# Work buffers for weight sums in a fused attention, mixture-of-experts and Strassen kernel, and idle turnings ahead of its branches

## The chip, the cores and the metric

The kernel runs on one core of one Trainium2 chip. The metric is the device time of one execution in microseconds (us). A core has five engines with a queue of instructions each: TensorE (PE in the profile; PEld is its loading of weights), VectorE (DVE), ScalarE (ACT), GpSimd (POOL) and SyncE (SP, which mostly issues DMAs). An engine takes its instructions strictly in order and waits at one until the semaphores that it names have come. DVEq, ACTq and PEq in the profile are the instruction sequencers of these engines, which do branches, register loads and the issuing of DMAs.

## The reference

Three stages in a row, all in float32 (cut to what is computed):

```python
# 1. attention in chunks of 64 tokens, 8 batches x 8 heads, 576 tokens each, head size 64
x = softmax(q_c @ k_c.T / 8) @ v_c            # -> 4608 tokens x 512
# 2. eight experts; only tokens with x @ w_skip > 0 are computed
e_idx = argmax(xc @ w_gate); gate = softmax(xc @ w_gate)[e_idx]
for e in range(8):                            # w1[e]: 512 x 1024, w2[e]: 1024 x 512
    y[mask] = gate * (relu(xc[mask] @ w1[e]) @ w2[e])
x[do_compute] = xc + y
# 3. a maxout layer: w1, w2, w3 are 512 x 768, w_out is 768 x 512
h = max(relu(x @ w1), x @ w2, x @ w3)
return h @ w_out
```

How many tokens an expert gets is known only on the chip.

## The kernel before

Every float32 product is made of three matmuls (`mm3`): each operand is split into a high part `hi` and a rest `lo` of a reduced type, and hi·hi, hi·lo and lo·hi are added up in PSUM. For the weights of expert e the raw piece `raw_e` is loaded by SP, ScalarE casts it to `whi_e` (L90), and VectorE, or GpSimd for pieces 0 and 1, subtracts to get `wlo_e` (L91). There are eight pieces for each expert. Pieces 0, 1, 2, 3 and 7 of expert e+1 (`EARLY`) are written ahead of expert e's products, pieces 6, 4 and 5 (`LATE`) after its branch.

Phase 1 (to about 213 us of the trace) is attention and the sorting of tokens to experts. Phase 2 (213 to 530 us) runs the experts 0 to 7, here called e0 to e7. An expert does two tiles of 128 tokens without a question (`first_tiles`: 96 matmuls `h`, of 256 columns, that make the hidden layer; 12 turnings `trm`, transposes through TensorE that prepare the rows of the next tiles; then 48 matmuls `y` back). VectorE's put-back (L694, `xg<-y,xg`) ends a tile, and GpSimd writes its rows home. Then stands a branch, `tc.If(n_e > 256)` (L983; L989 for e7): a third tile (`single`) is done only if the expert has so many tokens, inside of it a fourth (L916), and inside of that a loop (L920, L921). [...] The third tile of e0 is done always. In the profiled execution the third tile was done by e0, e2, e3, e5 and e7, and the fourth by e2 and e3.

Phase 3 (530 to 1108 us) is the maxout layer in blocks of 1024 rows, with seven products of sums of weight quarters in place of eight. These sums (`n_q`, kept in DRAM as `m_sums`) are 18 steps called n_q0 to n_q17. Steps 0 to 10 are made during phase 2, beside the experts (`STEPS = [2, 2, 2, 2, 2, 1, 0, 0]` of them are written in e0 to e7), and 11 to 17 in the first block of phase 3. A step loads one raw block (`n_raw`, two buffers), narrows it from 64-bit to 32-bit values (L531 to L533 and L536 on VectorE, L534 on ScalarE), makes four sums (L569 to L572 on VectorE, 128x128), casts (L575 on ScalarE) and subtracts (L576 on VectorE, 128x896), and then ScalarE and SP each store one half (L577, L578). The buffer `n_q` of phase 2 is one (`bufs=1`), so that the first instructions of a step (L531, L534) wait until the store of the step before has landed. In the first block `m2_direct` narrows w_out in six pieces (`n_q_m`), with the buffers "s4" (two) that steps 11 to 17 use as well.

The order of the instructions on each engine comes from a scheduler that goes by the order of the program text and by the buffers that are free; the kernel pins some of it with `issue_after`.

## Time and profile before

| what | value |
|---|---|
| time, median of 3 runs | 1114.9 us (1110.21 to 1116.59) |
| the profiled execution: its time / its span | 1109.83 / 1108.1 us |
| mean granted clock of TensorE | 0.979 of full speed |
| busy share of the span: PE, DVE, ACT, POOL | 94%, 55%, 40%, 28% |
| phase 2, the eight experts | about 213 to 530 us |
| phase 3 | about 530 to 1108 us |

TensorE is at work in nearly all of the span. What can be won is where it stands still, and where it runs at half clock after it stood still. The averages over the whole span say little of single stages: VectorE, 55% busy over all, is 89% busy (23.11 of 26.00 us) in the stretch of expert e4.

### The profile page before, as it was taken

What the parts mean: (1) busy time and instruction counts of PE and PEld (TensorE: products, weight loads), DVE (VectorE), ACT (ScalarE), POOL (GpSimd) and SP (SyncE); (2) the same over time, 40 slices, a digit from 0 to 9 for tenths busy, and PEclk for the clock granted to TensorE, in tenths of its full rate; (3) what the DMA queues carried; (4) which work ended last, traced back from release to release, by engine and by line L of the source; (5) the groups of instructions that cost most, each with busy time, mean ns of one, the idle gap of its engine ahead of it and who ended that gap; (6) DMA issues with size and microseconds to landing.
All of it is one profiled execution on the core that took longest, in us unless ns stands there. A gap on an engine that the chain in (4) does not pass through costs nothing.

```text
span 1108.1 us, 17499 instructions
## 1 busy us (share of the span) xinstructions
PE 1042.2 (94%) x6320; PEld 872.1 (79%) x6320; DVE 614.8 (55%) x1299; ACT 446.2 (40%) x774; POOL 309.1 (28%) x297
## 2 busy tenths in 40 slices
PE   7899799988899998998899799999999999999997
PEld 6788677777788787887687588878888888788996
DVE  6687588756756477671499772335244442443241
ACT  6677487434434244431444342222322232223231
POOL 4124232364404044320432160222312140123021
PEclk9999799999899999999999999999999999999999
DMA  9999996257764468544898934663566545666591
GB/s 211 195 216 232 261 229 183 89 195 259 265 217 136 138 211 273 192 150 141 274 319 285 300 114 136 197 190 114 165 194 192 166 139 166 183 186 208 186 288 38
DMA packets 217513, 216.99 MB, mean 196 GB/s; under 512 B 50219, under 2 KB 179403, under 8 KB 217408
## 3 DMA queue, kind: packets, MB, share of 16 engines
q1 hardware_dynamic: 206384, 183.62, 57.3%
q0 software_dynamic: 8432, 23.76, 6.6%
q10 hardware_dynamic: 2592, 8.26, 1.9%
q8 instruction: 60, 0.98, 0.4%
q14 instruction: 45, 0.37, 0.1%
HBM read 175.15 MB, written 41.83 MB: 196 GB/s over the span
## 4 chain that ended last, share of the span: by engine, by line
PE 41%; DMA 6%; DVE 3%; issue 3%; POOL 1%; ACT 0%; SPq 0%; POOLq 0%; DVEq 0%; ACTq 0%
PE f_a L705 5%; PE f_a L707 5%; PE f_a L706 5%; PE o L705 4%; PE o L707 4%; PE o L706 4%; DMA ws<-m_sums 3%; PE f_d L705 3%; PE f_d L707 3%; PE f_d L706 3%; DMA m_sums<-n_q 2%; PE f_b L705 1%; PE f_b L707 1%; PE f_b L706 1%; PE trf L879 1%
## 5 line engine op out<-in xcount | busy, mean ns | idle before, releaser
L91 POOL TENSOR_TENSOR fh<-best,fh 128x512 fp32r<-128x512 f32 (+1 forms) x60 | 77.0, 1290 | 356.3 <-ACT fh L90 270.4
L705 PE MATMUL f_a<-x_t,ws 128*128 128x512 f32 (+1 forms) x270 | 100.7, 373 | 5.0 <-DVE p L1034 4.8
L706 PE MATMUL f_a<-x_t,ws 128*128 128x512 f32 (+1 forms) x270 | 99.9, 370 | 0.0
L707 PE MATMUL f_a<-x_t,ws 128*128 128x512 f32 (+1 forms) x270 | 99.7, 370 | 0.0
L90 ACT CAST whi_e<-raw_e 128x1024 fp32r<-128x1024 f32 x64 | 65.1, 1045 | 60.0 <-DMA raw_e<-in_moe_w_dram 34.8
L705 PE MATMUL h<-xhi,whi_e 128*128 128x256 f32 x256 | 75.5, 295 | 12.2 <-DVEq L983 7.0
L706 PE MATMUL o<-wlo_m,fh 128*128 128x512 f32 x216 | 84.6, 392 | 0.0
L705 PE MATMUL o<-whi_m,fh 128*128 128x512 f32 x216 | 83.4, 392 | 0.0
L707 PE MATMUL o<-whi_m,fh 128*128 128x512 f32 x216 | 83.4, 392 | 0.0
L91 DVE TENSOR_TENSOR wlo_e<-raw_e,whi_e 128x1024 fp32r<-128x1024 f32 x50 | 67.1, 1351 | 18.1 <-ACT whi_e L90 15.9
L705 PE MATMUL y<-whi_e,hhi 128*128 128x512 f32 x184 | 74.3, 406 | 2.6 <-ACT hhi L772 1.8
L707 PE MATMUL y<-whi_e,hlo 128*128 128x512 f32 x184 | 72.8, 400 | 1.8 <-DVE hlo L712 1.6
L706 PE MATMUL h<-xlo,whi_e 128*128 128x256 f32 x256 | 74.4, 291 | 0.0
L707 PE MATMUL h<-xhi,wlo_e 128*128 128x256 f32 x256 | 74.3, 290 | 0.0
L706 PE MATMUL y<-wlo_e,hhi 128*128 128x512 f32 x184 | 72.3, 395 | 0.0
L696 POOL DMA_INDIRECT x_dram<-xg,ids_sb x20 | 20.6, 1030 | 180.2 <-DVE xg L694 72.8
L90 ACT CAST fh<-best 128x512 fp32r<-128x512 f32 (+1 forms) x60 | 34.7, 579 | 89.5 <-DVE best L1036 57.9
L1039 ACT COPY p<-f_a 128x512 f32<-128x512 f32 (+1 forms) x45 | 24.5, 545 | 99.3 <-PE f_a L707 99.1
L705 PEld LDWEIGHTS h<-xhi,whi_e 128*128 128x128 f32 x256 | 51.0, 199 | 15.3 <-ACTq L983 6.3
L705 PEld LDWEIGHTS f_a<-x_t,ws 128*128 128x128 f32 x270 | 51.2, 190 | 14.5 <-DVE p L1034 5.3
L707 PEld LDWEIGHTS f_a<-x_t,ws 128*128 128x128 f32 x270 | 51.2, 190 | 8.6
L706 PEld LDWEIGHTS f_a<-x_t,ws 128*128 128x128 f32 x270 | 51.2, 190 | 8.3
(226 smaller groups left out, 2678.7 us busy)
## 6 DMA issues: line engine op xcount, KB each, us to landing
ws<-m_sums SPq DMA_DIRECT2D x135, 512.0 KB, 5.2
raw_e<-in_moe_w_dram SPq DMA_DIRECT2D x64, 512.0 KB, 5.1
ws<-m_sums SPq DMA_DIRECT2D x45, 256.0 KB, 3.9
v_bd<-in_v_dram SPq DMA_DIRECT2D x144, 64.0 KB, 4.2
x<-x_dram SPq DMA_DIRECT2D x36, 256.0 KB, 4.9
out_dram<-os SPq DMA_DIRECT2D x36, 256.0 KB, 2.0
x_dram<-xg SPq DMA_DIRECT2D x17, 512.0 KB, 4.2
m_sums<-n_raw ACTq DMA_DIRECT2D x18, 448.0 KB, 6.0
```

The lines of the kernel that those rows point to most:

```text
L90: nc.scalar.copy(hi, src),
L91: eng.tensor_tensor(lo, src, hi.bitcast(F32), op=ALU.subtract),
L696: ins = nc.gpsimd.indirect_dma_start(out=x_dram[:, :], out_offset=bass.IndirectOffsetOnAxis(ap=ids, axis=0), in_=xg, in_offset=None, bound ...
L705: nc.tensor.matmul(acc, ahi, bhi, start=first, stop=False, skip_group_check=onto)
L706: nc.tensor.matmul(acc, ahi, blo, start=False, stop=False, skip_group_check=onto)
L707: return nc.tensor.matmul(acc, alo, bhi, start=False, stop=last, skip_group_check=onto)
L879: nc.tensor.transpose(tr[:, i * P:(i + 1) * P], row[:, c * P:(c + 1) * P], ident)
L1039: nc.scalar.copy(p1, acc_a)
```

## The change

It has four parts. `n_q` of phase 2 gets two buffers. To make room, the raw pieces of weights that go through the pool `mpool` have one buffer in place of two, and piece 1 goes through the other pool, whose three buffers it shares with pieces 2, 7 and `LATE`. The narrowing of w_out (`m2_direct`) gets a buffer of its own, one, in place of the two of "s4". And after the last `y` matmul ahead of each branch TensorE does eight turnings of the constant `ident` into a PSUM tile that nobody reads (`ahead_of_branch`): after the second tile of e1 to e7 and after each `single`, but not after e7's last one.

```diff
-        raw = (pool or rpool).tile([P, 1024], F32, tag="raw", name=f"raw_{name}", bufs=2 if pool else 3)
+        raw = (pool or rpool).tile([P, 1024], F32, tag="raw", name=f"raw_{name}", bufs=1 if pool else 3)
...
-            quarters = mpool.tile([P, 8, P], F32, tag="n_q", name=f"n_q{i}", bufs=1)
+            quarters = mpool.tile([P, 8, P], F32, tag="n_q", name=f"n_q{i}", bufs=2)
...
-    def second(name, key, hhi, hlo, i, xg, ids, tag=None):
+    def second(name, key, hhi, hlo, i, xg, ids, tag=None, ahead_of_branch=False):
...
-                mm3(acc, hhi[:, kf, sl], hlo[:, kf, sl], bhi[:, kf % 2, :], blo[:, kf % 2, :], n == 0, n == 7)
+                done = mm3(acc, hhi[:, kf, sl], hlo[:, kf, sl], bhi[:, kf % 2, :], blo[:, kf % 2, :], n == 0, n == 7)
+        if ahead_of_branch:
+            busy = ps_tr(f"busy_{name}")
+            with tc.issue_after(done.ins):
+                for n in range(8):
+                    nc.tensor.transpose(busy[:, n % 4 * P:n % 4 * P + P], ident, ident)
         put_back(key, xg, ids, acc)
...
-            second(f"{name}_{i}", (e, i), hhi, hlo, i, xgs[i], idss[i], "tr" if e == 0 else None)
+            second(f"{name}_{i}", (e, i), hhi, hlo, i, xgs[i], idss[i], "tr" if e == 0 else None,
+                ahead_of_branch=e > 0 and i == 1)
...
-        second(name, key, hhi, hlo, 0, xg, ids)
+        second(name, key, hhi, hlo, 0, xg, ids, ahead_of_branch=key != (E - 1, 2))
...
-        quarters = four_kb([P, 8, P], F32, f"n_q_m{m}_{f}_{half}", True)
+        quarters = fpool.tile([P, 8, P], F32, tag="n_q_m", name=f"n_q_m{m}_{f}_{half}", bufs=1)
...
-                    raw = load_raw(*expert_src(e + 1, i), mpool if i in (0, 1, 3) else None)
+                    raw = load_raw(*expert_src(e + 1, i), mpool if i in (0, 3) else None)
```

The diff doesn't show how instructions move. Three places follow.

First, VectorE at the end of e0's third tile, ahead of the branch L916 (L922 after the change). `n_q0` and `n_q1` are the first two steps, `hlo_0_2` and `xlo_1` belong to the tiles, and the names in brackets are the semaphores that an instruction waits for. Before:

```order
L576 TENSOR_TENSOR n_q0_3949<-n_q0_3949,n_raw0_3947 128x896 [waits Activation_49]
L518 TENSOR_TENSOR xlo_1_4264<-trm_1_0_4265,xhi_1_4263 128x4x128 [waits Activation_49]
L773 TENSOR_TENSOR hlo_0_2_4218<-trh_0_2_1_4249,hhi_0_2_4217 128x512 [waits DMAHW2_49,Activation_49]
L773 TENSOR_TENSOR hlo_0_2_4218<-trh_0_2_0_4256,hhi_0_2_4217 128x512 [waits Activation_49]
L518 TENSOR_TENSOR xlo_1_4264<-trm_1_1_4272,xhi_1_4263 128x4x128 [waits Activation_49]
L531 TENSOR_SCALAR n_q1_3965<-n_raw1_3963 128x512 [waits DMAHW7_49,DMAHW6_49,DVE_49]
L532 SCALAR_TENSOR_TENSOR n_q1_3965<-n_raw1_3963,n_q1_3965 128x512 [waits DVE_49]
L694 SCALAR_TENSOR_TENSOR xg_0_3687<-y_0_2_4279,xg_0_3687 128x512 [waits DMAHW5_49,DMASW2_49,PE_49]
L533 SCALAR_TENSOR_TENSOR n_q1_3965<-n_raw1_3963,n_q1_3965 128x512 [waits DVE_49]
```

After:

```order
L572 TENSOR_TENSOR n_q0_3949<-n_q0_3949 128x128 [waits DVE_49]
L779 TENSOR_TENSOR hlo_0_2_4218<-trh_0_2_0_4256,hhi_0_2_4217 128x512 [waits Activation_49]
L572 TENSOR_TENSOR n_q1_3965<-n_q1_3965 128x128 [waits DVE_49]
L576 TENSOR_TENSOR n_q0_3949<-n_q0_3949,n_raw0_3947 128x896 [waits Activation_49]
L518 TENSOR_TENSOR xlo_1_4264<-trm_1_1_4272,xhi_1_4263 128x4x128 [waits Activation_49]
L576 TENSOR_TENSOR n_q1_3965<-n_q1_3965,n_raw1_3963 128x896 [waits Activation_49]
L694 SCALAR_TENSOR_TENSOR xg_0_3687<-y_0_2_4279,xg_0_3687 128x512 [waits DMASW2_49,PE_49]
```

Both steps now end ahead of the branch, and the start of n_q1, which waits for a DMA, no longer stands next to the put-back. In the same manner e1 holds n_q2 and n_q3 whole, where it held n_q2 and the end of n_q1 (from L536 on).

Second, VectorE ahead of e4's branch. `wlo_e5` are pieces of e5's weights, `xlo_5` the turned rows of e5. Before, step n_q7 stands there, and of n_q6 only its last instruction, L576, further ahead in e4:

```order
L518 TENSOR_TENSOR xlo_5_6337<-trm_5_1_6345,xhi_5_6336 128x4x128 [waits Activation_49]
L571 TENSOR_TENSOR n_q7_5707<-n_q7_5707 128x128 [waits DVE_49]
L91 TENSOR_TENSOR wlo_e5_7_6176<-raw_e5_7_6173,whi_e5_7_6175 128x1024 [waits DMAHW2_49,Activation_49]
L572 TENSOR_TENSOR n_q7_5707<-n_q7_5707 128x128 [waits DVE_49]
L694 SCALAR_TENSOR_TENSOR xg_0_3687<-y_4_0_6352,xg_0_3687 128x512 [waits DMASW2_49,PE_49]
L576 TENSOR_TENSOR n_q7_5707<-n_q7_5707,n_raw7_5705 128x896 [waits Activation_49]
L694 SCALAR_TENSOR_TENSOR xg_0_3687<-y_4_1_6381,xg_0_3687 128x512 [waits DMASW4_49,PE_49]
L973 TENSOR_LOAD cnt_i_130 x2
L983 COMPARE_AND_BRANCH
```

After, e4 holds all of n_q8 and n_q9, and more of its other work stands late:

```order
L518 TENSOR_TENSOR xlo_5_6472<-trm_5_1_6480,xhi_5_6471 128x4x128 [waits Activation_49]
L572 TENSOR_TENSOR n_q9_6388<-n_q9_6388 128x128 [waits DVE_49]
L91 TENSOR_TENSOR wlo_e5_2_6299<-raw_e5_2_6296,whi_e5_2_6298 128x1024 [waits DMAHW5_49,Activation_49]
L91 TENSOR_TENSOR wlo_e5_3_6305<-raw_e5_3_6302,whi_e5_3_6304 128x1024 [waits DMAHW6_49,Activation_49,Pool_49]
L694 SCALAR_TENSOR_TENSOR xg_0_3687<-y_4_0_6487,xg_0_3687 128x512 [waits DMASW2_49,PE_49]
L576 TENSOR_TENSOR n_q9_6388<-n_q9_6388,n_raw9_6386 128x896 [waits Activation_49]
L91 TENSOR_TENSOR wlo_e5_7_6311<-raw_e5_7_6308,whi_e5_7_6310 128x1024 [waits DMAHW7_49,Activation_49]
L694 SCALAR_TENSOR_TENSOR xg_0_3687<-y_4_1_6516,xg_0_3687 128x512 [waits DMASW4_49,PE_49]
L979 TENSOR_LOAD cnt_i_130 x2
L989 COMPARE_AND_BRANCH
```

So the steps move forward by up to two: e3 has n_q6 and n_q7, e5 has only n_q10 (before: n_q8 and n_q9), and e6 has none (before: n_q10).

Third, TensorE ahead of e1's branch, `y_1_1` being the second tile. Before:

```order
L705 MATMUL y_1_1_4743<-whi_e1_5_4316,hhi_1_4541 128x512
L706 MATMUL y_1_1_4743<-wlo_e1_5_4317,hhi_1_4541 128x512
L707 MATMUL y_1_1_4743<-whi_e1_5_4316,hlo_1_4542 128x512
L973 TENSOR_LOAD cnt_i_130 x2
L983 COMPARE_AND_BRANCH
```

After:

```order
L706 MATMUL y_1_1_4770<-wlo_e1_5_4326,hhi_1_4568 128x512
L707 MATMUL y_1_1_4770<-whi_e1_5_4325,hlo_1_4569 128x512
L729 MATMUL busy_1_1_4795<-ident_77 128x128 [waits DVE_49]
L729 MATMUL busy_1_1_4795<-ident_77 128x128 x7
L979 TENSOR_LOAD cnt_i_130 x2
L989 COMPARE_AND_BRANCH
```

The eight turnings stand between the last `y` matmul and the branch; the put-back on VectorE waits for the matmul and not for them.

## Rows read from the trace of the kernel before

**Rows 1.** Waits of TensorE: engine, line, releaser, us in total, times, longest us.

```profile
PE h L705 <- DVEq L983: 7.0, 3, 3.8
```

**Rows 2.** Timeline of TensorE: start, duration, instruction, in brackets idle before and releaser.

```profile
261.30 0.39 PE L705 MATMUL h<-xhi,whi_e 128*128 128x256 f32 x1 [2.81 <-ACTq L916]
...
290.59 0.55 PE L705 MATMUL h<-xhi,whi_e 128*128 128x256 f32 x1 [3.78 <-DVEq L983]
...
343.94 0.36 PE L705 MATMUL h<-xhi,whi_e 128*128 128x256 f32 x1 [0.82 <-PEq L920]
...
420.27 0.36 PE L705 MATMUL h<-xhi,whi_e 128*128 128x256 f32 x1 [1.73 <-DVEq L983]
...
462.74 0.36 PE L705 MATMUL h<-xhi,whi_e 128*128 128x256 f32 x1 [0.55 <-PEq L916]
...
488.17 0.36 PE L705 MATMUL h<-xhi,whi_e 128*128 128x256 f32 x1 [1.47 <-DVEq L983]
```

**Rows 3.** Windows: stretch, us, busy us of PE, PEld, DVE, ACT, POOL, PEclk, DMA, GB/s.

```profile
262.70:266.00 3.30, 3.30 (x17) 3.30 (x17) 3.19 (x5) 1.71 (x3) 2.69 (x3) 0.51 0.28 82
289.90:297.30 7.40, 6.71 (x34) 6.75 (x35) 4.65 (x6) 5.72 (x7) 5.50 (x5) 0.54 0.99 315
420.30:424.00 3.70, 3.70 (x31) 3.70 (x32) 0.00 (x0) 0.77 (x1) 1.28 (x3) 1.00 0.97 363
440.00:443.30 3.30, 2.80 (x7) 2.22 (x8) 3.30 (x4) 3.30 (x6) 0.00 (x0) 0.50 1.00 358
```

**Rows 4.** Timelines of ScalarE and VectorE from the end of e0 through e1.

```profile
260.14 0.67 ACT L534 ACTIVATE n_q<-n_raw 128x512 f32<-128x512 f32 x1 [6.07 <-DMA m_sums<-n_q]
...
262.81 0.69 DVE L536 SCALAR_TENSOR_TENSOR n_q<-n_q 128x512 f32<-128x512 f32 x1 [0.25 <-DVEq L916]
...
276.83 1.23 DVE L91 TENSOR_TENSOR wlo_e<-raw_e,whi_e 128x1024 fp32r<-128x1024 f32 x1 [1.85 <-ACT whi_e L90]
...
283.19 0.43 DVE L531 TENSOR_SCALAR n_q<-n_raw 128x512 int32<-128x512 int32 x1 [1.61 <-DMA m_sums<-n_q]
...
288.51 1.09 DVE L576 TENSOR_TENSOR n_q<-n_q,n_raw 128x896 fp32r<-128x896 f32 x1 [1.05 <-ACT n_raw L575]
289.52 0.74 DVE L694 SCALAR_TENSOR_TENSOR xg<-y,xg 128x512 f32<-128x512 f32 x1
```

**Rows 5.** Timelines of VectorE and TensorE in expert e5.

```profile
426.34 0.43 DVE L531 TENSOR_SCALAR n_q<-n_raw 128x512 int32<-128x512 int32 x1 [6.28 <-DMA m_sums<-n_q]
...
436.41 0.50 PE L705 MATMUL y<-whi_e,hhi 128*128 128x512 f32 x1 [0.29 <-ACT hhi L711]
...
438.78 0.50 PE L707 MATMUL y<-whi_e,hlo 128*128 128x512 f32 x1 [1.64 <-DVE hlo L712]
...
440.50 0.80 PE L705 MATMUL y<-whi_e,hhi 128*128 128x512 f32 x1 [0.52 <-ACT hhi L711]
```

**Rows 6.** Timeline of TensorE: turnings in e2, and at the start of the program.

```profile
304.84 1.47 PE L514 MATMUL trm<-ident,xg 128*128 128x128 f32 x12
...
1.55 2.61 PE L129 MATMUL warm<-ident 128*128 128x128 f32 x11 [1.55 <-POOL ident masks.py:199]
...
6.79 0.66 PE L241 MATMUL trqk_True<-ident,qr 128*128 128x128 f32 x4 [0.17 <-ACT qr L227]
```

**Rows 7.** Expert e4: the window of all engines, and timelines of VectorE and GpSimd.

```profile
394.00:420.00 26.00, 24.17 (x156) 21.72 (x156) 23.11 (x26) 13.39 (x18) 13.19 (x10) 1.00 0.79 270
...
404.77 5.68 DVE L532 SCALAR_TENSOR_TENSOR n_q<-n_raw,n_q 128x512 int32<-128x512 int32 x1
...
405.18 4.72 POOL L91 TENSOR_TENSOR wlo_e<-raw_e,whi_e 128x1024 fp32r<-128x1024 f32 x2
```

**Rows 8.** First block of phase 3: timelines of VectorE and TensorE.

```profile
613.15 1.55 DVE L531 TENSOR_SCALAR n_q_m<-raw_m 128x512 int32<-128x512 int32 x1 [1.90 <-DMA m_sums<-n_q]
...
621.34 0.80 PE L705 MATMUL f_a<-x_t,ws 128*128 128x512 f32 x1 [4.84 <-DVE p L1034]
...
626.07 0.50 PE L705 MATMUL f_a<-x_b,ws 128*128 128x512 f32 x1 [1.80 <-DMA ws<-m_sums]
```

## The prediction

> **What bounds the kernel now.** TensorE is at work in nearly all of the span, so I first read what it waits for, by engine and line, and then the timeline at each of these places. The change touches phase 2 and the first block of phase 3, and there the reader is to see three things.
>
> One: the longest waits of phase 2 stand at branches that are not taken, where the next expert's first `h` matmul comes late [rows 1, 2]. They differ: 0.55 and 0.82 us where TensorE's own sequencer is last, 1.47 and 1.73 where VectorE's is (a put-back, then its branch), but 2.81 ahead of e1 and 3.78 ahead of e2.
>
> [...] Work at half clock costs half of its busy time: 3.30 / 2 = 1.65, 6.71 / 2 = 3.35, and 1.65 us again (the last stretch is 3.30 long; its 0.5 of idle is in the next sum, so this is 0.25 too much, which I let stand).
>
> Three: who made them late. Ahead of e1 ScalarE stood 6.07 us at the start of step n_q1, until n_q0's store had landed, and only then came to its branch. In e1 VectorE waited 1.61 us for the store of n_q1, and worked until its put-back at 289.52, though TensorE's last `y` ends at about 286.8 [rows 4]. In e5 the same wait took 6.28 us on VectorE; `hlo` behind it was late, and TensorE stood 0.29 + 1.64 + 0.52 = 2.45 us [rows 5]. One buffer is the cause of all three.
>
> **The change, part by part.** I count against the profiled execution, 1109.83 us; the median of the runs is 1114.9, so 5.1 us come on top at the end.
>
> *A, gap ahead of e1.* With both steps started early and ended ahead of the branch, nothing on ScalarE waits; what is next late is VectorE's put-back and branch, 1.47 to 1.73 in the other rows. I take 1.6: 2.81 - 1.6 = 1.2 saved.
>
> *B, the length of e1.* From its first `h` to that of e2 it is 290.59 - 261.30 = 29.29 us [rows 2]. TensorE's own work in an expert at full clock is that of e6: 488.17 - 1.47 - 462.74 = 23.96 us [rows 2]; with a gap of 1.6 the least is 25.6. But VectorE is the one that ends e1. From 262.81 to the end of the last put-back at 290.26 are 27.45 us, with idle times of 0.25, 1.85, 1.61 and 1.05 [rows 4], so 22.7 of work. After the change e1 does both steps whole: L531, L532 and L533 once more, 0.43 + 0.69 + 0.69 = 1.8 us (the first from [rows 4], the others by L536's 0.69 there, which has the same shape), so 24.5. Of the idle time the 0.25 and 1.61 go, while the waits for ScalarE, 1.85 and 1.05, may stay or be filled. With 0.33 from the put-back to the first `h`: 24.8 to 27.7, at least 25.6. I take the middle, 26.6: 2.7 saved (1.6 to 3.7). Half of the gain of the second buffer is thus lost to VectorE's own load; the slow clock at e1's start goes too, and is inside this term.
>
> *C, the clock at the start of e2.* The gap left is 26.6 - 23.96 = 2.6, of which the eight turnings fill 0.87 (see E), so TensorE stands about 1.8 us: near to the 1.73 that kept the clock, under the 2.81 after which it fell for 3.3 us. I give it half of 1.65: of 3.35 lost before, 0.8 stays, 2.5 saved (0 to 3.35).
>
> *D, the stall of e5.* e5 has one step in place of two and no store to wait for: 2.45 + 1.65 = 4.1 saved. At the least the 1.64 that goes to `hlo`, with nothing of the clock; ScalarE's two short waits may come from late weights.
>
> *E, the turnings.* Twelve of them took 1.47 us, four 0.66 [rows 6]: eight are 0.98 by the share, and 0.81 by the difference, which leaves out the tail of the last. I take 0.87. In this data the marked places are reached 13 times. Five branches are taken (after e2's first and third tile, e3's, e5's first): there TensorE runs on without a gap, so all is on the path, 5 x 0.87 = 4.4. Three not taken end with TensorE's sequencer or nearly so (after e2's and e3's fourth tile, e5's third; 0.82 and 0.55 in [rows 2]): 3 x 0.87 = 2.6. The other five (e0's third tile, e1, e4, e6, e7) wait for VectorE, and the turnings lie beside its put-back, of 0.74, and branch: 0.87 + 0.55 to 0.82 is 1.4 to 1.7 against 1.47 to 1.73, so 0 to 0.2, together 0.2. Sum: 7.2 lost. Ends: 4.4 if only taken branches pay; 10.0 if at these the sequencer's lead over the matmuls, behind which a branch hides now, is lost with the shorter turnings, and 0.55 comes on top five times (7.1 + 2.6 + 0.3).
>
> [...]
>
> *F, e4.* This is what the change worsens. VectorE is busy 23.11 of the 26 us of e4 [rows 7], with n_q7 and the last instruction of n_q6. After, it has two whole steps: L531, L532, L533, L536 (0.43 + 3 x 0.69 = 2.5) and four short sums of about 0.2, 3.4 us more. If all of its 2.9 idle takes that up, 0.5 is late; if none, 3.4. GpSimd's two subtractions held one VectorE instruction for 5.68 us [rows 7], so the middle of e4 takes nothing up, and what is moved stands behind it. The early waits for ScalarE can be filled. I take 1.4 (0.5 to 3.4). With the gap of 1.73 there now, less the turnings, TensorE would stand 2.3 us, and again I give half of 1.65 for the clock (0 to 3.35): 2.2 lost.
>
> e2 and e3 get two whole steps as well, but there a third tile follows without a gap: the `h` of that tile needs nothing of VectorE's tail, which has some 5.7 us of cover there: 24 matmuls of twice the columns of those of which 31 took 3.70 us [rows 3].
>
> *G, the first block of phase 3.* With a buffer of its own the first narrowing needn't wait 1.90 us for a store, nor stretch to 1.55 [rows 8]. For that the whole of it now stands ahead of the end of n_q17, four instructions of about 0.6, and the second one's start, which waits for its raw block, stands ahead of n_q17's L576. TensorE's waits of 4.84 and 1.80 hang on that tail [rows 8]. Six narrowings run one after the other in one buffer. From 3 saved (1.90 + 1.12) to 4 lost (four instructions and the wait): I take 0.5 lost.
>
> *The raw buffers*: piece 3 still waits for piece 0's GpSimd subtraction, as now; piece 1 is loaded once the last expert's late pieces are cast, ahead of its use. Nothing, while the loads stay some us early.
>
> Sum: - 1.2 - 2.7 - 2.5 - 4.1 + 7.2 + 2.2 + 0.5 = - 0.6, so 1109.2 for the profiled execution and 1114.3 for the median.
>
> **The rivals.** *VectorE keeps pace and the turnings hold the clock* (faster): B 3.7, C 3.35, E 4.4, F 0.5, the rest as above: - 1.2 - 3.7 - 3.35 - 4.1 + 4.4 + 0.5 + 0.5 = - 6.95, 1108.0. For it: the idle left at e1 and e4 is near to the 1.73 that kept the clock, and VectorE has idle time in both. Against it: VectorE is 89% busy in e4, and taken branches have nothing to hide turnings behind.
>
> *VectorE becomes the bound at the ends of e1 and e4* (slower). Two whole steps in an expert without a third tile: the put-back stands last in VectorE's queue, so TensorE stands over 2.8 us at both ends and falls to half clock for long. B 1.6, C 0, F 3.4 + 3.35: - 1.2 - 1.6 - 4.1 + 7.2 + 6.75 + 0.5 = + 7.6, 1122.5. It decides from a VectorE tail of about 2 us behind the last `y` at both. For it: e1 already ends this way. Against it: the waits that spread it are gone.
>
> [...]
>
> *It doesn't do what it says*: loads or stores in flight hold the steps as one buffer did, A to D are not had, and E and G are paid: + 7.7, 1122.6.
>
> **How the numbers follow.** A measurement of this kernel can tell about 0.5%, 5.6 us, from no change. Forecast (net near zero) 0.43; faster rival 0.32; VectorE rival 0.15; turnings' rule 0.05; not as said 0.05. [...] So faster 0.33, same 0.46, slower 0.21. The range: the low end is the faster rival with 3 of G and some 1 for the median's own scatter, 1104; the high end is the two slower ones at 1122. Only what is beyond these is left out. The likeliest case alone reaches from 1109 to 1119.
>
> **What would show it.** Right: no wait for `m_sums<-n_q` on ScalarE ahead of e1, on VectorE in e1 or e5; 1.6 us ahead of e1, and 2.6 ahead of e2 with VectorE last; no stall of `y` in e5; eight turnings of 0.87 us with no gap behind them at taken branches; a gap over 2.5 after e4. Wrong: if turnings at taken branches cost nothing or 1.4 each, if VectorE ends e4 in time, if half clock stays at e2's start, or if the waits of the first block grow by more than 2 us.

## The result

The changed kernel takes 1129.1 us at the median, beside 1115.7 us for the kernel before: a ratio of 1.0114, with a 95% interval of 1.0078 to 1.0149. Measured twice more, each time beside the kernel before on one chip, it was 10.6 us slower (1128.9 against 1118.3) and 11.6 us slower (1117.8 against 1106.2; ratio 1.0112, 1.0065 to 1.0160). So it is slower by about 1%. The forecast was 1114.3 us, with a range up to 1122: the time is outside the range, and on the side that had a chance of 0.21.

Chips differ by 1%: the kernel before had medians of 1106.2 and 1106.9 on one chip, 1117.9 and 1118.3 on two others. So kernels are compared below on the same chip, and stages by their lengths and not by their place in the span.

The waits that the change was to remove are gone from phase 2. Waits of ScalarE and VectorE (engine, line, releaser; us in total, times, longest) for the stores of the work buffer, in the kernel before:

```profile
ACT n_q L534 <- DMA m_sums<-n_q: 31.0, 10, 6.1
...
DVE n_q L531 <- DMA m_sums<-n_q: 20.1, 8, 6.3
```

and in the changed kernel:

```profile
ACT n_q L534 <- DMA m_sums<-n_q: 5.2, 5, 3.5
...
DVE n_q L531 <- DMA m_sums<-n_q: 2.0, 2, 1.2
```

What is left of them lies in the first block of phase 3, at 584 to 616 us.

But TensorE waits longer than before at its branches, and no longer for VectorE. Its waits in the changed kernel (PEq is TensorE's own sequencer; L989 and L995 are the lines that were L983 and L989):

```profile
PE h L705 <- PEq L989: 9.8, 3, 5.5
PE f_a L705 <- DVE p L1040: 4.7, 1, 4.7
...
PE h L705 <- PEq L995: 2.2, 1, 2.2
```

The first row stands where [rows 1] had 7.0 us for VectorE's sequencer, and it is 9.8 although eight turnings now fill 0.87 us of each of the three gaps. The timeline of TensorE, changed kernel, at the places of [rows 2] (start, duration, instruction, idle before it with its releaser):

```profile
270.92 0.36 PE L705 MATMUL h<-xhi,whi_e 128*128 128x256 f32 x1 [0.40 <-PEq L922]
...
298.30 0.36 PE L705 MATMUL h<-xhi,whi_e 128*128 128x256 f32 x1 [2.53 <-PEq L989]
...
352.59 0.35 PE L705 MATMUL h<-xhi,whi_e 128*128 128x256 f32 x1 [0.54 <-PEq L926]
...
428.98 1.03 PE L729 MATMUL busy<-ident 128*128 128x128 f32 x8
435.52 0.55 PE L705 MATMUL h<-xhi,whi_e 128*128 128x256 f32 x1 [5.51 <-PEq L989]
...
476.29 0.36 PE L705 MATMUL h<-xhi,whi_e 128*128 128x256 f32 x1 [0.54 <-PEq L922]
...
502.88 0.36 PE L705 MATMUL h<-xhi,whi_e 128*128 128x256 f32 x1 [1.76 <-PEq L989]
```

From the end of the last `y` (0.87 us before the end of the turnings) to the next `h` these are 1.28, 3.41, 1.42, 6.38, 1.42 and 2.63 us, where [rows 2] had 2.81, 3.78, 0.82, 1.73, 0.55 and 1.47. Only the first two became shorter. The clock behind them, in windows of the changed kernel (columns as in [rows 3]: the number before the last two is the granted clock):

```profile
298.30:303.30 5.00, 5.00 (x29) 5.00 (x30) 2.45 (x2) 3.32 (x4) 2.18 (x3) 0.66 1.03 388
352.59:357.59 5.00, 5.00 (x42) 5.00 (x43) 3.56 (x5) 3.78 (x5) 3.00 (x3) 1.00 0.36 109
435.52:440.52 5.00, 5.00 (x27) 5.00 (x28) 2.36 (x2) 2.07 (x3) 3.50 (x3) 0.60 0.91 297
502.88:507.88 5.00, 5.00 (x29) 5.00 (x30) 3.60 (x4) 3.42 (x4) 0.00 (x0) 0.66 0.14 51
```

TensorE does 27 to 29 matmuls in the 5 us at e2, e5 and e7, and 42 where it has the full clock. In [rows 3] the clock after e4 was 1.00; now it is 0.60 in the first 5 us of e5.

VectorE, which the forecast took for the last one after e4, is done early. Its timeline there, changed kernel:

```profile
429.08 1.22 DVE L91 TENSOR_TENSOR wlo_e<-raw_e,whi_e 128x1024 fp32r<-128x1024 f32 x1
430.22 0.74 DVE L694 SCALAR_TENSOR_TENSOR xg<-y,xg 128x512 f32<-128x512 f32 x1
436.62 1.23 DVE L91 TENSOR_TENSOR wlo_e<-raw_e,whi_e 128x1024 fp32r<-128x1024 f32 x1 [5.66 <-ACT whi_e L90]
```

The last put-back ends at 430.96, and TensorE's `h` starts 4.6 us later. What held TensorE in these 4.6 us is its own branch, as the instructions of line L989 around e4 show (engine or sequencer, operation; ns min/median/max; first and last start), changed kernel:

```profile
L989 PEldq COMPARE_BRANCH  x1: 6715/6715/6715, 428.6 to 428.6; - x1
L989 DVEq COMPARE_BRANCH  x1: 74/74/74, 430.0 to 430.0; - x1
```

and the same branch in the kernel before, L983 around e4:

```profile
L983 PEldq COMPARE_BRANCH  x1: 4029/4029/4029, 415.2 to 415.2; - x1
L983 DVEq COMPARE_BRANCH  x1: 69/69/69, 419.4 to 419.4; - x1
```

The last `y` there, in the kernel before:

```profile
418.16 0.39 PE L707 MATMUL y<-whi_e,hlo 128*128 128x512 f32 x1
```

Before, the branch was long as well (4.03 us), but began at 415.2, 3.4 us ahead of the end of the last `y` at 418.55, so most of it lay beside the matmuls. After the change it takes 6.72 us and begins 0.5 us ahead (428.6 against 429.14). The experiments below ask why it begins late, why it is long, and what the other parts cost.

### The profile page after: what moved, and what is told of

It reads as the page before. It is cut to its first block, busy times and chain, and to the rows that moved or that the text cites. A ratio compares the mean times of both kernels' runs of the same rounds, so it can differ in the third digit from the quotient of the medians.

```text
span 1129.2 us, 17688 instructions
## 1 busy us (share of the span) xinstructions
PE 1059.0 (94%) x6424; PEld 887.3 (79%) x6424; DVE 603.8 (53%) x1299; ACT 445.4 (39%) x774; POOL 311.0 (28%) x297
## 3 DMA queue, kind: packets, MB, share of 16 engines
q8 instruction: 62, 1.02, 0.4%
## 4 chain that ended last, share of the span: by engine, by line
PE 42%; DMA 6%; DVE 2%; issue 1%; POOL 1%; ACT 1%; SPq 0%; POOLq 0%; ACTq 0%; DVEq 0%
PE f_a L705 5%; PE f_a L707 5%; PE f_a L706 5%; PE o L706 4%; PE o L707 4%; PE o L705 4%; DMA ws<-m_sums 3%; PE f_d L705 3%; PE f_d L706 3%; PE f_d L707 3%; PE f_b L705 1%; PE f_b L707 1%; PE f_b L706 1%; DMA m_sums<-n_raw 1%; PE trf L885 1%
## 5 line engine op out<-in xcount | busy, mean ns | idle before, releaser
L91 DVE TENSOR_TENSOR wlo_e<-raw_e,whi_e 128x1024 fp32r<-128x1024 f32 x50 | 63.8, 1296 | 26.7 <-ACT whi_e L90 25.1
L696 POOL DMA_INDIRECT x_dram<-xg,ids_sb x20 | 24.3, 1215 | 159.9 <-DVE xg L694 98.1
```

The costliest lines, as they stand in the source:

```text
L91: eng.tensor_tensor(lo, src, hi.bitcast(F32), op=ALU.subtract),
L696: ins = nc.gpsimd.indirect_dma_start(out=x_dram[:, :], out_offset=bass.IndirectOffsetOnAxis(ap=ids, axis=0), in_=xg, in_offset=None, bound ...
```

## The experiments

The theory after the result ("lead theory" in the expectations): the two `n_q` buffers bring what was forecast, and the turnings take more away than that, at the four branches that jump over the code of a whole tile that is not done (the far branches, behind the first two tiles of e1, e4, e6 and e7), by way of TensorE's sequencer. Its lead is how long it begins such a branch before TensorE's last `y` ends. Rival theories: VectorE is late because of the moved steps; the narrowing's own buffer costs the time in phase 3; the difference lies in the first phase, where the two first profiles differ by 11.7 us.

**The parts alone.** Against the changed kernel, no turnings:

```
-        if ahead_of_branch:
+        if False:
```

> The changed kernel with its buffers but without the eight turnings ahead of the branches. Lead theory (TensorE's sequencer reaches the branches that skip a third tile only 0.4 to 1.2 us ahead of the last y matmul instead of 3, and the branch itself takes 3.7 us and more): all of phase 2's loss goes, the gaps at 298.3, 435.5, 502.9 and 530.5 fall to 1.5 to 3 us, the half clock behind e6 and e7 goes, and the time falls by 12 to 18 us to 1111 to 1117, a ratio to before of 0.996 to 1.001. Buffer theory (the other buffers or the moved steps are what makes it slower, in phase 1 too, which was 11.7 us longer in the profile): the time stays at 1122 to 1129, ratio 1.006 to 1.012.

Measured: 1.0001 (0.9974 to 1.0028), 1116.2 us, as the lead theory had it. So the turnings cost about what the whole change does, and the rest comes to nothing.

Against the changed kernel, the turnings only:

```
-        ... tag="raw", name=f"raw_{name}", bufs=1 if pool else 3)
+        ... tag="raw", name=f"raw_{name}", bufs=2 if pool else 3)
-            quarters = mpool.tile(... tag="n_q", name=f"n_q{i}", bufs=2)
+            quarters = mpool.tile(... tag="n_q", name=f"n_q{i}", bufs=1)
-        quarters = fpool.tile([P, 8, P], F32, tag="n_q_m", name=f"n_q_m{m}_{f}_{half}", bufs=1)
+        quarters = four_kb([P, 8, P], F32, f"n_q_m{m}_{f}_{half}", True)
-                    raw = load_raw(*expert_src(e + 1, i), mpool if i in (0, 3) else None)
+                    raw = load_raw(*expert_src(e + 1, i), mpool if i in (0, 1, 3) else None)
```

> The kernel before with the eight turnings alone. Lead theory: five taken branches at 1.03 us, three near ones at about 1, the far ones of e1, e4, e6 and e7 1 to 3 us each and 1.65 us of half clock behind those of e6 and e7: 1126 to 1132, ratio 1.010 to 1.015. Buffer theory: 1116 to 1120, ratio 1.000 to 1.004, the eight turnings themselves at the five taken branches being all that counts.

Measured: 1.0068 (1.0033 to 1.0103). Alone they cost 7.6 us by the ratio and 4.9 by the medians, less than the 1.010 to 1.015 of the lead theory and more than the rival's 1.000 to 1.004. That this is near to the forecast's 7.2 is chance, for the sites are others: the four far gaps grew from 8.6 to 12.1 us, as the table further down shows.

Against the kernel before, two `n_q` buffers only, with the raw buffers that make room for them:

```
-        ... tag="raw", name=f"raw_{name}", bufs=2 if pool else 3)
+        ... tag="raw", name=f"raw_{name}", bufs=1 if pool else 3)
-            quarters = mpool.tile(... tag="n_q", name=f"n_q{i}", bufs=1)
+            quarters = mpool.tile(... tag="n_q", name=f"n_q{i}", bufs=2)
-                    raw = load_raw(*expert_src(e + 1, i), mpool if i in (0, 1, 3) else None)
+                    raw = load_raw(*expert_src(e + 1, i), mpool if i in (0, 3) else None)
```

> The kernel before with two n_q buffers and the raw buffers that pay for them, nothing else. Lead theory, and the prediction's terms A to D and F: 4 to 8 us less than before, ratio 0.993 to 0.997, and a phase 1 that is as long as before within a few us. Buffer theory: 1122 to 1128, ratio 1.006 to 1.011, with a phase 1 that is longer by about 10.

Measured: 0.9906 (0.9873 to 0.9938), 1109.0 us, 8.9 under the kernel before beside it. The gap ahead of e1 is 0.45 us, the length of e5 39.09 in place of 42.47. This is a little more than the expected 4 to 8 us, and this part alone beats both kernels.

Against the kernel before, the narrowing's own buffer only:

```
-        quarters = four_kb([P, 8, P], F32, f"n_q_m{m}_{f}_{half}", True)
+        quarters = fpool.tile([P, 8, P], F32, tag="n_q_m", name=f"n_q_m{m}_{f}_{half}", bufs=1)
```

> The kernel before with a buffer of its own for the narrowing of w_out, nothing else. The prediction's term G: 3 less to 4 more, ratio 0.997 to 1.004; the wait of 1.90 for n_q's store ahead of the first narrowing is gone. Buffer theory: a ratio of 1.004 or more would put a part of the loss here.

Measured: 1.0032 (1.0005 to 1.0059). A small loss of 3.6 us, inside the range that was expected, where the forecast had 0.5.

**The form and the place of the turnings.** Against the changed kernel, four matmuls of 512 columns in place of the eight turnings, for the same 0.9 us:

```
-                for n in range(8):
-                    nc.tensor.transpose(busy[:, n % 4 * P:n % 4 * P + P], ident, ident)
+                for n in range(4):
+                    nc.tensor.matmul(busy, hhi[:, 0, sl], bhi[:, 0, :], start=True, stop=True)
```

> The changed kernel, but with four idle matmuls of 512 columns (4 x 0.227 = 0.91 us of TensorE) in place of the eight turnings (0.88 us): the same TensorE time, half as many instructions in its queue; nobody reads them. Lead theory: what counts is how far the sequencer is ahead of the array when it meets the branch; it is so many instructions ahead, so with long ones it meets the far branches 3 us ahead of the last idle matmul, as it did 3 us ahead of the last y. The four far gaps (e1, e4, e6, e7), from the last y to the next h, come down from 3.4, 6.4, 2.6 and 3.1 us to 1 to 3; the time to 1120 to 1125, ratio 1.003 to 1.007. Time theory (the turnings cost only what they take on TensorE, and the long branch of e4 is chance): as after, 1.009 to 1.014, and the branches start as late as there.

Measured: 1.0045 (1.0022 to 1.0068), so 7 us better than turnings of the same length. This looks like a matter of the form of the idle work, but the branches differ too: at e4 the branch took 0.33 us and the gap was 1.06, not 6.4, while at e1, where the branch took 5.15 us, the gap stayed 3.73. The run doesn't tell the two apart. The last experiments do for e4: there eight turnings ahead of a short branch leave a gap of 1.02.

Against the changed kernel, turnings only behind single tiles:

```
-                ahead_of_branch=e > 0 and i == 1)
+                ahead_of_branch=False)
```

> The changed kernel with the eight turnings only behind third and fourth tiles (six places in this data, whose branches jump a short way or are taken). Lead theory: TensorE's branch there takes 0.2 to 0.4 us and starts early enough; two taken at 0.88 and four not taken at 0.5 to 0.9: 4 to 5 us over no_turnings, ratio to before 1.002 to 1.006. Time theory: six of 13 places, so 6/13 of 12.9 us = 6 us, ratio 1.005 to 1.007.

and only behind the first two tiles:

```
-        second(name, key, hhi, hlo, 0, xg, ids, ahead_of_branch=key != (E - 1, 2))
+        second(name, key, hhi, hlo, 0, xg, ids, ahead_of_branch=False)
```

> The changed kernel with the eight turnings only behind the first two tiles of e1 to e7 (seven places: three taken, four that jump over the whole third tile). Lead theory: the four jumps lose 0.4 to 5 us each and the half clock behind them 1.65 each: 8 to 12 us over no_turnings, ratio to before 1.007 to 1.011, and TensorE's branches start 0.5 to 1.4 us ahead of the last y. Time theory: 7/13 of 12.9 us = 7 us, 1.005 to 1.007.

Measured: 1.0048 (1.0017 to 1.0079) behind single tiles and 1.0013 (0.9989 to 1.0036), where no turnings at all have 0.9985 on the same chip. So 7 and 3 us by the ratios, 10 together, where both cost 12 to 14. The 3 us lie below what either theory had for the far sites (7 to 12); of the four branches there only two were long in this kernel, those of e4 and e7 took 0.43 and 0.34 us. The trace of the first is of more use than its time: at e6, where it has no turnings ahead of the branch, the branch took 4.60 us, and 0.32 us in the kernel before.

Against the kernel with two `n_q` buffers, the narrowing's buffer own for one half and shared for the other:

```
-        quarters = four_kb([P, 8, P], F32, f"n_q_m{m}_{f}_{half}", True)
+        quarters = (
+            four_kb([P, 8, P], F32, f"n_q_m{m}_{f}_{half}", True) if half else
+            fpool.tile([P, 8, P], F32, tag="n_q_m", name=f"n_q_m{m}_{f}_{half}", bufs=1))
```

> The kernel before with two n_q buffers, and the narrowing of w_out through a buffer of its own for its first halves and through the s4 buffers, as before, for its second halves: two can be in work at a time. Serial theory (with the one buffer the six narrowings run one after the other, the last ends at about 655 us, where VectorE owes the next block its first rows, and TensorE stands 1.8 us there): the waits at the start of the second block go, and the time is within 0.2% of that with two n_q buffers alone, ratio to before 0.989 to 0.994. Order theory (it is the moved first narrowing that delays n_q17): the wait for ws stays long and the ratio is 0.996 to 1.002, as with the one buffer.

Measured: 0.9950 (0.9920 to 0.9980), between 0.9985 for one own buffer and 0.9937 for the shared ones on that chip. Two buffers in turn win most of it back by the mean, which agrees with a loss by too few buffers, but the interval reaches into the ranges of both theories.

**Both kernels again on one chip, and VectorE.** The kernel before and the changed one, unchanged:

> The kernel before, unchanged, once more. In its first profile the time from the start to the first h of the first branch step was 213.2 us, in the profile of the changed kernel 224.9 us, though the order of instructions is the same until about 200 us; the kernels of the first experiments had 224 to 229 us, those of the next four 212 to 217 us. Theory that this belongs to the chip or the execution: this run's length agrees with those of the two other kernels beside it within some 5 us, and from that first h to the end it takes 897 to 903 us as the first profile did. Rival, that the change lengthens the first phase: here 211 to 215 us, and the changed kernel beside it 222 us or more.

> The changed kernel, unchanged, paired in five rounds on one chip. The record has 1.0114 of the time before, over runs that were not all on one chip. Singles so far: two n_q buffers -10.5 us, the narrowing's own buffer alone +3.6, the turnings alone +7.6; the first two together 0.0. Theory that part of the 1.0114 is a difference between chips: ratio 1.003 to 1.009 (0.0 and the turnings' 1.3 to 7.6 us, a little more). Rival, that the three parts hurt each other: 1.010 to 1.013, 11 to 15 us.

Measured: the kernel before had its first `h` of e0 at 226.8 us and the changed one at 227.4, so the difference of 11.7 us between the first two profiles is of the chip or the execution. But the medians beside each other are 1118.3 and 1128.9 us, 0.94% apart, and the ratio on record for this run is the same 1.0114 (1.0078 to 1.0149) as for the first comparison. So a difference between chips is at most a small part of the 1%.

Against the kernel with two `n_q` buffers, other experts for the background steps:

```
-    STEPS = [2, 2, 2, 2, 2, 1, 0, 0]
+    STEPS = [2, 1, 2, 2, 1, 2, 1, 0]
```

> Two n_q buffers only, and the background steps of the eight branches dealt as 2, 1, 2, 2, 1, 2, 1, 0, so that the branch steps with five experts' worth of weight sums in e1 and e4 have one background step and VectorE has less beside them. Theory that VectorE is last at the end of e1: the gap of TensorE between e1 and e2, 3.09 us with a clock of 0.50 behind it in the kernel with two n_q buffers, falls to 1.0 to 1.7 us with a clock of 1.00 behind it, and the ratio is 0.985 to 0.990. Rival, that TensorE's own far branch is last there anyway: the gap stays above 2.5 us and the ratio is 0.990 to 0.994.

Measured: the theory's gap came, its time did not. Between e1 and e2 TensorE stood 1.28 us, not 3.09, and the clock of the first 5 us of e2 was 1.00 and not 0.50. Window, other steps:

```profile
299.29:304.29 5.00, 5.00 (x42) 5.00 (x43) 1.23 (x1) 2.35 (x3) 2.68 (x4) 1.00 0.98 327
```

and two `n_q` buffers only:

```profile
299.33:304.33 5.00, 5.00 (x23) 5.00 (x24) 2.45 (x2) 2.11 (x3) 2.17 (x3) 0.50 1.02 383
```

So VectorE is the last one at the end of e1, as the forecast had it in its term B. But e3 and e5 became 1.0 and 1.5 us longer, and from the first `h` of e0 to the first `f_a` it takes 305.6 us, against 304.8 with two `n_q` buffers only: the time is 0.9934 (0.9910 to 0.9958), the rival's. VectorE's load was moved, not removed.

**The turnings moved ahead, and all of it on one chip.** Against the changed kernel, the turnings stand behind the second of the eight matmul triples and not behind the last, so that TensorE has 18 matmuls of 512 columns between them and the branch:

```
+        last = None
...
-                done = mm3(acc, ...)
-        if ahead_of_branch:
-            busy = ps_tr(f"busy_{name}")
-            with tc.issue_after(done.ins):
-                for n in range(8):
-                    nc.tensor.transpose(busy[:, n % 4 * P:n % 4 * P + P], ident, ident)
+                with tc.issue_after(last.ins) if last else nullcontext():
+                    done = mm3(acc, ...)
+            if ahead_of_branch and n == 1:
+                busy = ps_tr(f"busy_{name}")
+                with tc.issue_after(done.ins):
+                    for j in range(8):
+                        last = nc.tensor.transpose(busy[:, j % 4 * P:j % 4 * P + P], ident, ident)
```

> The changed kernel with each group of eight turnings moved ahead by six of the eight matmul triples of the output sums, so that TensorE does the same number of the same instructions, of the same length and the same place in the program's size, but its last 18 instructions ahead of a branch are matmuls of 512 columns, as in the kernel before. Theory A, that TensorE's sequencer runs ahead by a number of instructions and so reaches the far branch late behind eight short ones: the four far not-taken branches take as long as in the changed kernel (3.3 to 6.7 us each, as they did in both of its profiles), but begin 2.5 to 3.5 us before the last y ends and not 0.5 to 1.5 us, the gaps at e1, e4, e6, e7 fall from 3.4 to 3.6, 6.1 to 6.4, 2.6, 3.1 us to about 3.1, 3.4, 1.6, 1.9 us, and the time falls by 4 to 7 us against the changed kernel beside it (ratio to it 0.994 to 0.997). Theory B, that the turnings cost their own 0.87 us and the clock, wherever they stand: the time is that of the changed kernel within 2 us.

Measured: 1.0075 (1.0042 to 1.0108), 1115.5 us, 2.3 under the changed kernel. The branches began 2.5 to 3.4 us ahead of the end of the last `y`, and the gaps at e1, e4, e6 and e7 were 2.42, 3.25, 1.41 and 1.97 us, near to what theory A said. The branch at e4 took 3.55 us, and not the 6.5 that it had expected. The time was not as it said: 2.3 us came of 4 to 7, and with 5 and 7 runs this is not clear of the noise, so that it can't decide against theory B. Of the 7.3 us by which the four gaps fell, 3.5 are the turnings themselves, which now stand ahead of the last `y`. That the rest of the cost stays with the turnings wherever they stand is an estimate: 13 groups of them are passed, 0.8 to 0.9 us each, so 10 to 12 us, and this kernel stands 10.1 us over the one without turnings. So the lead is shown, and its worth in time is not.

The changed kernel, the one without turnings and the one with two `n_q` buffers only, once more beside it:

> The changed kernel beside the others on one chip. Singles add to +0.7 us (two n_q buffers -10.5, own narrowing buffer +3.6, turnings +7.6), the kernel without turnings 0.1. If the turnings simply add, this stands 6 to 8 us over the kernel without turnings beside it; if they hurt each other, as the two measurements of this kernel (+10.6 and +12.7 us to before) suggest, 10 to 13 us over it.

> The changed kernel without the turnings, beside the kernel with two n_q buffers only, on one chip. Earlier 1.0001 and 0.9906 of before: 1.000 and 0.990 again, so 9 to 12 us apart, if the own single buffer of the narrowing costs that much once the weight sums have two buffers; 3 to 4 us apart, if it costs what it did alone (1.0032).

> Two n_q buffers only, again beside the others: ratio to before 0.988 to 0.993, the fastest of the four; if the first measurement was luck of the chip, 0.994 to 0.997, as the kernel with alternating narrowing buffers had on another chip.

Measured, medians on one chip: before 1106.2, two `n_q` buffers 1099.4 (0.9937, 0.9908 to 0.9967), with the narrowing's own buffer 1105.4 (0.9985, 0.9957 to 1.0012), with the turnings 1117.8 (1.0112). So - 6.8 + 6.0 + 12.4 = + 11.6. Two `n_q` buffers and the own buffer came out between the two values that had been expected for each. The turnings cost more on top of the other parts than alone (7.6 by the ratio, 4.9 by the medians), and the far gaps agree, 12.1 us alone and 15.5 to 16.3 in the changed kernel; for the own buffer (3.6 alone) the difference is not clear of the noise.

Where the own buffer costs: at the start of the second block of phase 3. Timeline of TensorE, changed kernel without turnings (the second run of it):

```profile
641.52 0.63 PE L885 MATMUL trf<-ident,x 128*128 128x128 f32 x4 [1.20 <-DVE x_b L891]
642.72 0.76 PE L885 MATMUL trf<-ident,x 128*128 128x128 f32 x4 [0.57 <-DVE t L906]
```

and of VectorE ahead of it:

```profile
635.36 1.67 DVE L532 SCALAR_TENSOR_TENSOR n_q_m<-raw_m,n_q_m 128x512 int32<-128x512 int32 x1
636.96 0.68 DVE L891 TENSOR_TENSOR x_b<-trf,x_b 128x512 fp32r<-128x512 f32 x1
637.56 0.67 DVE L899 TENSOR_TENSOR t<-t,trf 128x512 f32<-128x512 f32 x1
638.15 0.68 DVE L533 SCALAR_TENSOR_TENSOR n_q_m<-raw_m,n_q_m 128x512 int32<-128x512 int32 x1
...
640.68 1.29 DVE L891 TENSOR_TENSOR x_b<-trf,x_b 128x512 fp32r<-128x512 f32 x2
```

VectorE is still in the last of six narrowings (`n_q_m`) when TensorE wants the second block's `x_b`: one buffer makes them run one after the other, each waiting until the one before is used up. With the shared buffers VectorE is done with them when the block begins (two `n_q` buffers only, second run):

```profile
633.64 1.29 DVE L91 TENSOR_TENSOR wlo_m<-n_q_m,whi_m 128x512 fp32r<-128x512 f32 x2
634.90 0.69 DVE L885 TENSOR_TENSOR x_b<-trf,x_b 128x512 fp32r<-128x512 f32 x1
```

and TensorE has neither wait. From the first `f_a` to the last matmul that is 578.7 us against 571.3.

**The place of the code.** The far branches of twelve profiles, us of the branch on TensorE's sequencer, then the gap of TensorE from the last `y` to the next `h`:

| kernel | e1 | e4 | e6 | e7 |
|---|---|---|---|---|
| before | 3.76, 3.78 | 4.03, 1.72 | 0.32, 1.46 | 0.41, 1.59 |
| before, again | 4.54, 4.70 | 4.71, 1.70 | 0.32, 1.48 | 0.41, 1.60 |
| two `n_q`, second | 3.36, 2.60 | 4.65, 1.56 | 0.32, 0.30 | 0.41, 1.96 |
| no turnings, second | 4.71, 2.75 | 4.64, 1.55 | 0.32, 0.30 | 0.41, 1.96 |
| changed, first | 4.13, 3.41 | 6.72, 6.38 | 3.66, 2.63 | 3.68, 3.05 |
| changed, second | 4.63, 3.61 | 6.48, 6.13 | 3.70, 2.61 | 3.76, 3.13 |
| changed, third | 5.66, 4.65 | 6.56, 6.23 | 3.48, 2.67 | 3.32, 2.76 |
| turnings only | 3.65, 3.06 | 5.30, 4.06 | 3.54, 2.27 | 3.30, 2.67 |
| turnings ahead | 3.71, 2.42 | 3.55, 3.25 | 4.67, 1.41 | 3.31, 1.97 |
| four matmuls | 5.15, 3.73 | 0.33, 1.06 | 0.49, 1.21 | 3.61, 1.82 |
| only behind single tiles | 4.20, 2.56 | 5.05, 1.95 | 4.60, 1.54 | 0.32, 1.96 |
| only behind first two | 5.26, 4.24 | 0.43, 1.03 | 3.34, 2.28 | 0.34, 1.96 |

A far branch is short here (0.3 to 0.5 us) or long (3.3 to 6.7), and in the kernels profiled two or three times which of the two depended on the kernel and the site, and not on the execution. (At a nearer branch, the one behind e0's third tile, it did: L916 took 2.97 us in one profile of the kernel before and 0.53 in the other.) In the changed kernel the branch at e4 is the longest of all, 6.5 to 6.7 us; why it takes longer than the others is not shown. To see what decides, I made code longer that never runs, in the loop of `beyond` for tiles after an expert's fourth:

```
                     single(f"{e}_n", (e, 3), rows_T(f"{e}_n", [xg], t3), xg, ids)
+                    pad = ps_tr(f"pad_{e}")
+                    for n in range(8):
+                        nc.tensor.transpose(pad[:, n % 4 * P:n % 4 * P + P], ident, ident)
```

in the kernel with two `n_q` buffers (8, and 64 in a second one) and in the changed kernel (8):

> Two n_q buffers only, and eight transposes of 128 columns more in the loop body for tiles beyond the fourth of an expert, which runs for no expert here: TensorE executes the same instructions, only the program is longer by eight instructions per expert. In seven profiles without turnings the far not-taken branches of TensorE's sequencer took 3.3 to 5.0 us at e1 and e4, 0.32 at e6 and 0.41 at e7 (the last two to a hundredth or so), in the three of the changed kernel 4.1 to 5.7, 6.5 to 6.7, 3.5 to 3.7 and 3.3 to 3.8. Theory that the place of the code decides: at least one of e6 and e7 goes to 3.3 us or more here, or e1 or e4 to below 0.6. Rival, that what ran before decides: 3.3 to 5.0, 3.3 to 5.0, 0.32, 0.41 as without the pad. Time as with two n_q buffers alone in either case, since these branches begin 3 us early.

> The same with 64 transposes in the loop body that runs for no expert. By the theory of place the four durations are again others than without the pad, in some of the four; by the rival they are 3.3 to 5.0, 3.3 to 5.0, 0.32 and 0.41.

> The changed kernel with the eight transposes in the loop body that runs for no expert. Its far branches took 4.1 to 5.7, 6.5 to 6.7, 3.5 to 3.7 and 3.3 to 3.8 us in three profiles. By the theory of place at least one of them falls to below 0.6 us here or e4's leaves 6.4 to 6.8, and the gap of TensorE there follows it: a branch below 0.6 us leaves a gap of 1.0 to 1.3 us. By the rival they stay.

Measured, branch and gap at e1, e4, e6, e7: with 8 more 3.53 and 3.09, 0.42 and 0.64, 4.11 and 1.01, 3.93 and 1.96; with 64 more 3.51 and 2.91, 4.70 and 1.61, 4.10 and 1.00, 3.60 and 1.97; the changed kernel with 8 more 4.62 and 3.87, 0.42 and 1.02, 0.42 and 1.17, 0.33 and 1.58. The rival fell in all three: the executed instructions are the same (some turnings of the third tiles of e2 and e5 change places), and short became long and long short. In the changed kernel with the pad, L992 around e4:

```profile
L992 PEldq COMPARE_BRANCH  x1: 424/424/424, 427.2 to 427.2; - x1
```

where the same branch took 6.48 to 6.72 us without it. The four gaps add to 7.6 us there, against 15.5 to 16.3. But not all of the difference is won, for TensorE now stands still a little later, among the first `h` of e5, for 2.28 us in which it waits for nothing that the profile shows ("issue"):

```profile
433.66 0.39 PE L707 MATMUL h<-xhi,wlo_e 128*128 128x256 f32 x1 [2.28 <-issue]
```

The one execution took 1120.8 us beside 1119.8 for the kernel before, and 1107.6 and 1113.7 for the other two; single executions on one more chip, so their gain against the 1% is not measured closely.

The profile shows what goes with the long branches. One of the kinds of DMA queue in it is "instruction". In the stretch of the long branch at e4 of the changed kernel, 428.6 to 435.3, there are packets of it (queue and kind: packets, MB, share of 16 engines):

```profile
q8 instruction: 1, 0.02, 1.4%
q14 instruction: 1, 0.01, 0.6%
```

and in the stretch of the short one in the padded kernel, 427.2 to 427.65, the queues are these two alone:

```profile
q10 hardware_dynamic: 32, 0.06, 60.9%
q1 hardware_dynamic: 18, 0.04, 21.0%
```

It is so at the four far branches of all 20 profiles: one packet of the instruction queue q8, of 16 KB, lies inside each of the 53 long ones (3.3 to 6.7 us), and none inside any of the 27 short ones (0.3 to 0.5 us). In the longest, those at e4 of the changed kernel, it begins 3.8 to 4.0 us after the branch, in all others 0.9 to 2.9. By chance a stretch of 4 us would hold 0.3 of one, an estimate from the 25 that the kernel before has from 200 to 560 us. Such a packet, from 431.1 to 432.7, runs in the first part of the 2.28 us in the padded kernel too (431.4 to 433.7). With the pad, which changes little but the place of the code, the packets moved together with the long branches: one lies in the 4.11 us at e6, where the branch took 0.32 us without the pad, and none in the 0.42 us at e4 of the changed kernel. So the two come together; that the branch is long because of the packet is not shown. Which engine a packet belongs to the trace doesn't say.

## Why the prediction was wrong, by its own steps

*What bounds the kernel* was read rightly: the gaps at branches, the half clock behind the long ones (0.51 and 0.54, and 0.50 after the stall in e5 [rows 3]), and one buffer as the cause.

*A to D and F*, together - 8.3: measured - 6.8 and - 8.9 us in two medians, - 7.0 and - 10.5 by the ratios. Right in size. Of the terms: A, the gap ahead of e1, came to 0.40 to 0.45 us without turnings where I had 1.6, since the put-back is done in time there. But it was 0.41 in the second profile of the kernel before as well, so the loss that A was to save belonged to the one execution that I counted against. B, e1's length of 26.6, was 26.6 to 28.5 with VectorE last. C: half of the loss was to stay, with 0.87 us of turnings taken off the gap. That turnings count as work for the clock no run shows; without any, the clock in the first 5 us of e2 was 0.50 in one profile with two `n_q` buffers and 1.00 in the other. D, 4.1 for e5: its length fell by 3.0 to 3.5 without turnings. F, 2.2 lost in e4, did not come: the gap after e4 is 1.55 us without turnings, against 1.73 [rows 2]; VectorE took up the two steps.

*E, the turnings*: 7.2 forecast, 12.4 measured on one chip by the medians (14.0 by the ratios 1.0112 and 0.9985), above the upper end of 10.0. This is the step that failed, and within it the term for the far branches, 0.2 forecast and 9.8 measured. Its parts, from the third profile of the changed kernel and the second without turnings, on one chip: the five taken branches cost 5 x 0.79 = 4.0, as forecast (4.4). The timeline of TensorE in e2 of the changed kernel shows one, with no idle time behind:

```profile
323.84 1.04 PE L729 MATMUL busy<-ident 128*128 128x128 f32 x8
324.63 0.48 PE L705 MATMUL h<-whi_e,xhi 128*128 128x512 f32 x1
```

The four near branches (after e0's third tile and at the ends of e2, e3 and e5) have gaps of 1.28, 1.42, 1.42 and 1.42 against 0.40, 0.76, 0.78 and 0.94: 2.7, where I had 2.6 for three of them. But the four far ones, for which I had 0.2 together with e0's, "beside its put-back", have 4.65, 6.23, 2.67 and 2.76 against 2.75, 1.55, 0.30 and 1.96: 9.8 us. The sum is 16.4, and the eight lengths grew by 16.9; of that the rest of the program gave 4.4 back in these two executions and took 0.9 at the start.

What I overlooked: I read the gap's releaser, VectorE, as the limit, and costed TensorE's sequencer at the 0.55 to 0.82 us that it had at the near branches. At e1 and e4 its branch took 3.76 and 4.03 us already before; it could not be seen among the waits, since it began 3.4 us early and ended ahead of VectorE's (287.2 against 289.8 at e1, and only just at e4, 419.2 against 419.4). Eight short instructions behind the last `y` bring its start to 0.5 to 1.6 us ahead, so the hidden branch came to the surface. At e6 and e7 there was no long branch to hide before (0.32 and 0.41 us); there it became long, 3.3 to 3.8 us, with the new place of the code, of which no step of mine spoke. I named the lost lead as the upper end, but priced it at 0.55 for each (7.2 and five times 0.55 are 9.9; the three terms of that end are not the ones named).

The padded kernel shows how much of the miss hangs on the place of the code. With short branches at e4, e6 and e7 its far gaps are only 1.1 us over those of the kernel without turnings, so that E would come to 4.0 + 2.7 + 1.1 = 7.8, near to the 7.2 forecast, and to about 10 with the 2.28 us in e5. This rests on one execution on another chip. It took 1120.8 us beside 1119.8 for the kernel before, so by the luck of a layout the forecast of a net near zero might have come true, with the long branches still not in it.

*G, the first block*: 0.5 forecast, 3.6 measured alone, 6.0 and 7.3 on top of the two buffers; the upper end was 4. The mechanism was written down (six narrowings one after the other in one buffer), but I looked for its price in the first block alone, in the waits of [rows 8]; 4.7 and 1.2 us of those are there in the changed kernel too. The price came one block later, as 1.2 + 0.57 us for `x_b`, and in the clock: 0.83 and 0.96 in the two stretches of 25 us from 592.3 to 642.3 of the kernel without turnings (0.93 and 1.00 in those from 595.2 to 645.2 with two `n_q` buffers only); TensorE did 172 matmuls in the first pair and 196 in the second.

*The rivals*: that the change doesn't do what it says had the nearest time among them with 1122.6, but for a reason that did not hold, since the waits for stores went. VectorE as the bound fell at e4, where it ended in time; at the end of e1 it is the last one in the kernel with two `n_q` buffers. The faster rival, too, had the turnings at no more than 4.4. Whether turnings hold the clock (0.05 stood for a case in which they don't) stays open: behind the same gap after e6 (2.63 and 2.67 us, 0.87 of it turnings) the clock of the next 5 us was 0.66 in the first profile of the changed kernel and 1.00 in the third; without turnings a gap of 1.96 after e7 gave 0.66 in one kernel and 1.00 in another. Of the signs of being wrong two came: VectorE ended e4 in time, and e2's first 5 us still ran partly at half clock (0.66). The gap of over 2.5 us after e4, named as a sign of being right, came as 6.38, but by another cause.

*The sum* on one chip: - 6.8 + 6.0 + 12.4 = + 11.6, against - 8.3 + 0.5 + 7.2 = - 0.6.

## What to carry to other kernels

Before work is put in front of a branch, look at the sequencer's own records of that branch, not at the wait that the engine shows: a branch that is hidden, as the one of 4.03 us at e4 was behind VectorE's, costs nothing until what hides it is shortened. What stands directly ahead of the branch set here how early it began: 2.8 to 3.4 us ahead of the end of the last `y` behind `y` matmuls alone, 2.1 to 2.5 us with four matmuls of 512 columns behind them, 0.5 to 1.6 us with eight turnings of the same length together. Compare two kernels over more than one layout of their code before a difference of some us is given to the instructions that were changed. A buffer of its own with one place takes the overlap away that two shared ones gave, and the price is to be looked for where the queue that it lengthens ends.

## What the runs showed of the hardware

A far branch of TensorE's sequencer took 0.32 to 0.49 us or 3.3 to 6.7 us, and each of the 53 long ones had a packet of the instruction queue in it. Code that never runs changed which it was: with eight turnings more the one at e6 went from 0.32 to 4.11 us, and the one at e4 of the changed kernel from 6.5 to 0.42. At e6 and e7 it was 0.318 to 0.325 and 0.405 to 0.410 us in all nine profiles that have neither turnings nor pad, so this is a property of the program. Among these kernels, which differ by some instructions, a part of a difference of some us can be such a branch.

One of four chips ran the same kernels some 1% faster than the others (1106 against 1118 to 1120 us for the kernel before), most of it in the first phase: its first `h` of e0 came at 213 to 217 us in the kernels measured there, and at 223 to 229 us on the others.
